# First chunks' state scaling and diagonal sums on ScalarE, and another order of the first steps and loads, in a recurrence plus three-way maximum kernel

## The chip, the cores and the metric

The kernel runs on one core of one Trainium2 chip. The metric is the device time of one execution in microseconds (us), the median of several runs. Five engines run side by side, each through its own list of instructions in order, and wait for one another by semaphores: TensorE (PE, matmuls; PEld is its weight load), VectorE (DVE), ScalarE (ACT), GpSimd (POOL) and SyncE (SP). SyncE and ScalarE also issue the DMA transfers; "SPq" and "ACTq" in a row are such issues or waits in their queues.

## The reference

A gated linear recurrence over 768 time steps for 4 batches and 8 heads of 48 channels, whose output feeds a feed-forward stage:

```python
for t in range(S):
    kt, vt, rt, wt = (k[:, :, t], v[:, :, t], r[:, :, t], w[:, :, t])
    cur = np.einsum('bhd,bhe->bhde', u[None] * kt, vt)
    y[:, :, t] = np.einsum('bhd,bhde->bhe', rt, state + cur)
    state = wt[:, :, :, None] * state + np.einsum('bhd,bhe->bhde', kt, vt)
...
x = attn_out.transpose(0, 2, 1, 3).reshape(B * S, H * D)        # 3072 x 384
h = np.maximum(np.maximum(x @ w1, x @ w2), x @ w3)              # 3072 x 768
return h @ w_out                                                # 3072 x 384
```

## The kernel before

**Tiling.** The 4 x 768 time steps are cut into 24 chunks of 128 steps. Four chunks (512 tokens) make a "half", of which there are six, and the feed-forward stage works on one half at a time. The recurrence inside a chunk is turned into matmuls: a backward and a forward scan of the decays w over the chunk give factors by which k and r are scaled, products of the scaled r and k ("gram") are masked and multiplied with v, and a 48 x 48 state for each head carries over from chunk to chunk.

**Steps of a chunk k**, each one letter: `b` backward scan (and `dec`, a copy of its end values by ScalarE), `s` two small VectorE operations, `f` forward scan, `r` scales r and k, `c` a ScalarE check of the scan's result; `d` products of r and k for the diagonal, `D` their sums by TensorE into a PSUM tile, `e` copies the eight sums out of PSUM (`cs`) and lets GpSimd spread them on the diagonal of the tile `a` (two selections of 64 rows each), and issues the load of the v tile of chunk k+1; `X` the gram matmuls, `M` copies the masked gram into `a` on VectorE, `T` transposes of k and a ScalarE copy of them (`kn`), `R` the state's share of the output y, `U` the new state in PSUM, `S` the state times the next chunk's decays into `sstar`, `V` and `Z` the values in two halves, `E` copies y into the tile x on ScalarE. After chunk 2 `E` also issues six small DMAs that move rows inside x (three on SyncE's queue, three on ScalarE's), and again after chunk 3. `n` loads the 679 KB of a chunk's inputs in two transfers into one of three buffers. The v tiles have three buffers too, so the load for chunk 4 has to wait until TensorE has read the v tile of chunk 1 for the last time, in `Z` of chunk 1.

**Weights.** 24 tiles of 384 KB (64-bit numbers) come in by the step `w`. A tile is turned into 32-bit numbers in two parts: step `i` does the part of ScalarE (line 303), and VectorE follows with lines 312 and 314. `c` without a number and `p` do the same for the next tile in line, and `p` and `m` then run the matmuls of the feed-forward stage; the first two tiles are multiplied with 384 of the 512 tokens in `p` (line 147), and with the last 128 in `m` (line 155). From the third tile on `m` is line 167. The products of line 147 and 155, of `D`, and of line 167 take turns in three PSUM banks ("psm"); the third weight tile takes the bank that the ScalarE copy of line 130 empties.

**Order.** Nothing is reordered by a scheduler: every engine runs its instructions in the order in which the program writes them, and the string `FRONT` writes the first part, chunks 0 to 3 and the start of the feed-forward stage, by hand. `W` with a number is that many dummy matmuls. From chunk 4 on another string sets the order, and a loop lays chunks between the groups of feed-forward matmuls.

Of the kernel before, what the change touches and what calls it, by code (L numbers as in the profile page):

```python
# [34 lines left out]
ALU = mybir.AluOpType  # L35
AF = mybir.ActivationFunctionType
# [4 lines left out]
B, H, S, D = 4, 8, 768, 48  # L41
DM, FF = 384, 768
NP = 4
# [10 lines left out]
CPH = HT // C  # L54
# [12 lines left out]

FRONT = ("b0 s0 f0 d0 W2 D0 W3 r0 X0 T0 W3 c0 e0 b1 s1 d1 D1 U0 f1 W4 R0 e1 M0 V0 Z0 E0 S0 n3 r1 "  # L70
# [3 lines left out]
TURN = "b1 d1 w | f1 w | D1 r1 c1 | e1 M0 w | "  # L74
ORD = "w R0 V0 U0 X1 Z0 E0 b2 d2 | f2 n3 w | D2 S0 r2 c2 | e2 M1 w | T1 w | |"

# [18 lines left out]
def kernel(ctx: ExitStack, tc, tin, nat, u_flat, u_pair, v_t, w_all, out, ytr):  # L95
    nc = tc.nc
# [99 lines left out]
    with ExitStack() as fast:  # L196
# [23 lines left out]
        def load_nat(k):  # L220
            b, c = divmod(k, NCH)
            if k in natt:
                return
            vt = v_p.tile([128, DM], F32, name="v")
            kr = None
            if k >= CS:
                kr = nat_p.tile([128, 2, DM], F32, name="kr")
                nc.sync.dma_start(out=kr[:, :, :], in_=nat[b, c, :, 1:3, :])
            nc.sync.dma_start(out=vt[:, :], in_=nat[b, c, :, 0, :])
            natt[k] = (vt, kr)  # L230
# [39 lines left out]
        sstar = [cst.tile([128, NP, 64], F32, name=f"sstar{i}") for i in range(2)]  # L270
        dec = [cst.tile([128, LINE], F32, name=f"dec{i}")[:, 0:NP] for i in range(2)]
# [83 lines left out]
        prep = {k: {} for k in range(NK)}  # L355
# [59 lines left out]
        def prep_diag2(k):  # L415
            ahead("D", k)
            cs = small.tile([128, LINE], F32, name="cs")[:, 0:H]
            if k < CS:
                nc.vector.tensor_copy(out=cs[:, :], in_=prep[k]["ps"][:, 0:H])
            else:  # L420
                nc.vector.tensor_reduce(out=cs[:, :].rearrange("p (a b) -> p b a", a=2),  # L421
                                        in_=natt[k][1][:, 0, :].rearrange("p (b a d) -> p b a d", a=2, d=D),
                                        axis=AX.X, op=ALU.add)
            a = a_p.tile([128, 4, 3, HC], F32, name="a")
            for lo in (0, HC):
                rows = slice(lo, lo + HC)
                nc.gpsimd.affine_select(out=a[rows, :, 0:2, :], pattern=[[0, 4], [0, 2], [1, HC]],  # L427
                                        in_=cs[rows, :].rearrange("p (a b) -> p a b", b=2).unsqueeze(3).broadcast_to([HC, 4, 2, HC]),
                                        compare_op=ALU.is_equal, fill=0.0, base=0, channel_multiplier=-1)
            prep[k]["a"] = a  # L430
            if k + 1 < NK:
                load_nat(k + 1)
# [28 lines left out]
        def goes_on(k):  # L461
            return k % NCH < NCH - 1
# [36 lines left out]
        def state(k):  # L499

            if goes_on(k):
                new = prep[k]["pu"][0:112, 0:NP * D].rearrange("p (a b) -> p a b", a=NP)
                if k % NCH > 0 and k >= CPH:
                    cur = scur[0:112, :].rearrange("p (a b) -> p a b", a=NP)
                    nc.vector.tensor_tensor(out=cur, in0=new, in1=sstar[k % 2][0:112, :, 0:D], op=ALU.add)
                    new = cur
                nc.vector.tensor_tensor(out=sstar[(k + 1) % 2][0:112, :, 0:D], in0=new,
                                        in1=dec[(k + 1) % 2][0:112, :].unsqueeze(2).broadcast_to([112, NP, D]), op=ALU.mult)

        def after(later, sooner):  # L510

# [27 lines left out]
        def result(k):  # L539
# [11 lines left out]
            for lo in (0, 64) if cols else ():  # L551
                for j in range(KT):
                    eng = nc.scalar if lo and half < PLAIN else nc.sync
                    eng.dma_start(out=x[lo + 48:lo + 64, j, cols], in_=x[lo + 16 * j:lo + 16 * j + 16, KT, cols])  # L554

        steps = dict(X=scores, M=take, T=transposes, R=from_state, U=to_state, S=state, V=values, Z=values2, E=result, n=load,
                     b=prep_scan_b, s=prep_start, f=prep_scan_f, r=prep_rk, c=prep_check, d=prep_diag1,
                     D=prep_diag_sum, e=prep_diag2)
        ready = {("n", k) for k in range(3)}

        def ahead(step, k):

            if k < NK and (step, k) not in ready:
                ready.add((step, k))
                steps[step](k)
# [107 lines left out]
        def take_x(early=False):  # L673
            h = len(xs)
            there = ("E", CPH * (h + 1) - 2) in ready if early else units >= min(UPH * (h + 1) + XD, UPC * NK)
            if h < NH and there and groups >= GPH * h - 2 * CPH:
                xs[h] = x_parts(h)
# [39 lines left out]
        simple = dict(p=part, a=unit, c=weights, i=begin, w=load_w, m=group, f=fix, x=lambda: take_x(True))  # L717
        for step in FRONT.split():
            if step in simple:
# [14 lines left out]
    with tc.If(verdict[0] != 0, label="general"), ExitStack() as slow:  # L734
        pool = lambda name, bufs, **kw: slow.enter_context(tc.tile_pool(name=name, bufs=bufs, **kw))
        c1 = pool("c1", 1)
# [7 lines left out]
        with tc.For_i(0, B) as b:  # L744
            for pr in range(NP):
# [8 lines left out]
                for hh in range(2):  # L754
                    rows = slice(64 * hh, 64 * hh + 48)
                    for t, o in ((wt, pr * WS + 1), (rt, WC + pr * C), (kt, WC + NP * C + pr * C)):
                        for c in range(NCH):
                            for lo in (0, HC):
                                at = o + (HC - lo if t is kt and pr % 2 == 0 else lo)
                                nc.sync.dma_start(out=t[rows, c * C + lo:c * C + lo + HC],  # L760
                                                  in_=tin[ds(b, 1), c, rows, at:at + HC].rearrange("a p n -> (a p) n"))
                    nc.sync.dma_start(out=uc[rows, :], in_=u_pair[pr, hh])
                nc.vector.tensor_scalar(out=uk[0:112, :], in0=kt[0:112, :], scalar1=uc[0:112, :], scalar2=None, op0=ALU.mult)
                for j in range(KT):
                    with tc.For_i(0, 16) as i:
# [5 lines left out]
                        for hh in range(2):  # L771
                            nc.sync.dma_start(
                                out=vb[64 * hh:64 * hh + 48, :],
                                in_=v_t[ds(b, 1), 2 * pr + hh, ds(i + 16 * j, 1), :].rearrange("a e t -> (a e) t").broadcast_to([48, S]))
# [22 lines left out]
        for i in range(NW if w_all.dtype != F32 else 0):  # L797
# [5 lines left out]
            low, scale = raw[:, 0:2 * PC:2], sc[:, :].bitcast(F32)  # L803
# [16 lines left out]
        with tc.For_i(0, NH) as half:  # L820
            x = xs_p.tile([128, KT, HT], F32, name="x")
# [73 lines left out]
```

## Time and profile before

| | |
|---|---|
| time before, median of 3 runs (lowest to highest) | 417.63 us (417.21 to 419.69) |
| the profiled execution's own time | 414.51 us |
| its span in the trace | 412.8 us |
| TensorE busy in the span | 401.7 us (97%) |
| VectorE, ScalarE, GpSimd busy | 277.7, 151.4, 75.0 us |
| DMA bytes moved in the span | 53.30 MB |

The span runs from the first to the last instruction in the trace; 1.7 us of the profiled execution lie outside it. Busy times of engines overlap, so they don't add up; a matmul's end is modelled, so that a TensorE that is shown as busy may still be held up a little. Names such as `w`, `x`, `tin` are the program's tiles, L and a number a line of the kernel before.

### The profile page before, as it was taken

Reading aid. Unit: us, or ns where it says so; the run is one execution under the profiler, and the core shown is the slowest. Engines: PE = TensorE matmul, PEld = TensorE weight load, DVE = VectorE, ACT = ScalarE, POOL = GpSimd, SP = SyncE. Lnnn points to the kernel's source line nnn. Section 1 sums busy time; section 2 is a strip of 40 time slices with the busy share of each in tenths; the row PEclk is TensorE's granted clock in tenths of the full one; section 3 lists DMA queues with packets and bytes.
Section 4 is the critical chain, followed back from the end, with each engine's and each line's share of the span. In section 5 each row is a group of like instructions: output and inputs, shape, how many; then the busy total and the mean of one; then the engine's idle time right before and its main releaser. Section 6 shows DMA issues by size and latency. Waiting matters only on the chain.

```text
span 412.8 us, 9220 instructions
## 1 busy us (share of the span) xinstructions
PE 401.7 (97%) x3761; PEld 316.2 (77%) x3761; DVE 277.7 (67%) x515; ACT 151.4 (37%) x318; POOL 75.0 (18%) x92
## 2 busy tenths in 40 slices
PE   6989999999999999999999999999999999999995
PEld 3666454556688889988889988889988888978894
DVE  6999997878869959748877648777656622233320
ACT  1344333233525543525533635433622321412211
POOL 3311011033231311312221212322122200000000
PEclk9999999999999999999999999999999999999999
DMA  8695973641460321494564595751550000300002
GB/s 208 172 318 170 332 212 129 206 142 40 133 195 4 123 61 67 131 310 123 181 192 123 146 278 178 242 155 62 157 189 2 2 2 0 97 1 2 1 4 76
DMA packets 23838, 53.30 MB, mean 129 GB/s; under 512 B 3280, under 2 KB 9744, under 8 KB 23792
## 3 DMA queue, kind: packets, MB, share of 16 engines
q1 hardware_dynamic: 19872, 42.65, 34.0%
q10 hardware_dynamic: 3920, 10.03, 8.0%
q8 instruction: 30, 0.49, 0.5%
q14 instruction: 16, 0.13, 0.1%
HBM read 46.77 MB, written 4.72 MB: 125 GB/s over the span
## 4 chain that ended last, share of the span: by engine, by line
PE 89%; DVE 4%; DMA 2%; ACT 1%; issue 1%; ACTq 1%; SPq 1%; DVEq 0%; POOLq 0%
PE psm L167 56%; PE psm L187 16%; PE gram L449 4%; PE y L527 4%; PE tu L492 3%; PE y L482 2%; PE tu L469 2%; PE psm L147 1%; DMA out_dram<-m 1%; DVE gf L360 1%; DMA tin<-in_tin_dram 1%; ACTq L554 1%; PE psm L411 1%; DVE kr L399 1%; SPq L554 1%
## 5 line engine op out<-in xcount | busy, mean ns | idle before, releaser
L167 PE MATMUL psm<-x_hi,w 128*128 128x512 f32 x540 | 172.8, 394 | 0.2 <-ACT m L191 0.2
L167 PEld LDWEIGHTS psm<-x_hi,w 128*128 128x128 f32 x540 | 101.3, 188 | 22.3 <-ACT m L191 0.8
L167 PE MATMUL psm<-x_lo,w 128*128 128x512 f32 x270 | 105.3, 390 | 0.0
L133 DVE TENSOR_TENSOR m<-psm,m 128x512 f32<-128x512 f32 x60 | 41.1, 685 | 58.7 <-PE psm L167 42.4
L187 PE MATMUL psm<-w,h_hi 128*128 128x384 f32 x288 | 78.1, 364 | 0.0
L427 POOL TENSOR_SCALAR_AFFINE_SELECT a<-cs 64x512 f32<-64x512 f32 x48 | 36.1, 753 | 157.5 <-DVE cs L421 80.4
L167 PEld LDWEIGHTS psm<-x_lo,w 128*128 128x128 f32 x270 | 50.7, 188 | 9.8
L187 PEld LDWEIGHTS psm<-w,h_hi 128*128 128x128 f32 x288 | 51.7, 188 | 6.5 <-DVE w L314 0.4
L167 PE MATMUL psm<-x,w 128*128 128x512 f32 x96 | 43.1, 599 | 0.0
L545 ACT COPY x<-y 112x512 f32<-112x512 f32 x24 | 14.1, 587 | 76.3 <-PE y L527 75.9
L187 PE MATMUL psm<-w,h_lo 128*128 128x384 f32 x120 | 40.3, 335 | 0.0
L110 ACT CAST h_hi<-m 128x512 fp32r<-128x512 f32 x30 | 18.6, 622 | 54.8 <-DVE m L133 54.4
L391 ACT ACTIVATE gf<-gf 112x1034 f32<-112x1034 f32 x24 | 25.6, 1069 | 34.4 <-DVE tin L386 34.0
L374 DVE TENSOR_TENSOR_SCAN gf<-tin,d_fwd 112x517 f32<-112x517 f32 x24 | 36.5, 1519 | 0.7
L402 POOL TENSOR_TENSOR kr<-kr 128x384 f32<-128x384 f32 x16 | 17.9, 1119 | 92.6 <-PE y L527 76.7
L167 PEld LDWEIGHTS psm<-x,w 128*128 128x128 f32 x96 | 17.6, 190 | 19.5 <-issue 18.9
L360 DVE TENSOR_TENSOR_SCAN gf<-tin,d_bwd 112x517 f32<-112x517 f32 x24 | 29.9, 1246 | 3.7 <-DMA tin<-in_tin_dram 3.7
L111 DVE TENSOR_TENSOR h_lo<-m,h_hi 128x512 fp32r<-128x512 f32 x30 | 20.6, 688 | 17.0 <-ACT h_hi L110 17.0
L527 PE MATMUL y<-a,v 64*48 64x64 f32 (+3 forms) x768 | 25.7, 246 | 0.5
L458 DVE COPY_PREDICATED a<-mask,gram 128x384 f32<-128x384 int32 x48 | 25.3, 582 | 0.5 <-PE gram L449 0.5
L527 PEld LDWEIGHTS y<-a,v 64*64 64x64 f32 (+1 forms) x768 | 21.6, 126 | 4.7 <-issue 2.1
L130 ACT COPY m<-psm 128x512 f32<-128x512 f32 x30 | 17.5, 582 | 15.7 <-PE psm L167 11.0
(72 smaller groups left out, 422.7 us busy)
## 6 DMA issues: line engine op xcount, KB each, us to landing
tin<-in_tin_dram SPq DMA_DIRECT2D x23, 448.0 KB, 5.1
w<-in_w_all_dram SPq DMA_DIRECT2D x24, 384.0 KB, 7.2
cv<-in_w_all_dram ACTq DMA_DIRECT2D x24, 384.0 KB, 3.6
kr<-in_nat_dram SPq DMA_DIRECT2D x16, 384.0 KB, 5.5
tin<-in_tin_dram SPq DMA_DIRECT2D x23, 231.0 KB, 4.1
v<-in_nat_dram SPq DMA_DIRECT2D x24, 192.0 KB, 5.7
out_dram<-m SPq DMA_DIRECT2D x24, 192.0 KB, 2.3
x<-x SPq DMA_DIRECT2D x30, 32.0 KB, 2.0
```

The source lines that it names most:

```text
L110: nc.scalar.copy(out=hi, in_=src)
L111: rest = lambda: nc.vector.tensor_tensor(out=lo, in0=src, in1=hi.bitcast(F32), op=ALU.subtract)
L133: nc.vector.tensor_tensor(out=m[:, :], in0=ps[:, :], in1=m[:, :], op=ALU.max)
L167: nc.tensor.matmul(ps[:, :], lhsT=wt[f * 3 + wi][:, ct * 128:(ct + 1) * 128], rhs=xt[:, ct, :], start=(n == 0), stop=(n == KT * len(terms) ...
L187: nc.tensor.matmul(pss[tt][:, 0:DM], lhsT=ht[f][:, tok], rhs=wt[FT * 3 + f][:, :], start=(f == 0 and i == 0), stop=(f == FT - 1 and i == l ...
L360: nc.vector.tensor_tensor_scan(out=gf[0:112, 0, ::-1], data0=t[0:112, 0:WC][:, ::-1], data1=d_bwd[0:112, ::-1], initial=0.0, op0=ALU.mult, ...
L374: nc.vector.tensor_tensor_scan(out=gf[0:112, 1, :], data0=tbuf[k % NB][0:112, 0:WC], data1=d_fwd[0:112, :], initial=0.0, op0=ALU.mult, op1 ...
L391: nc.scalar.activation(out=flat, in_=flat, func=AF.Square, accum_out=acc[0:112, k:k + 1])
L402: nc.gpsimd.tensor_tensor(out=n[:, 0, :], in0=n[:, 0, :], in1=n[:, 1, :], op=ALU.mult)
L427: nc.gpsimd.affine_select(out=a[rows, :, 0:2, :], pattern=[[0, 4], [0, 2], [1, HC]], in_=cs[rows, :].rearrange("p (a b) -> p a b", b=2).un ...
L458: nc.vector.copy_predicated(out=p["a"][:, 2 * hh:2 * hh + 2, :, :].rearrange("p a b c -> p a (b c)"), mask=mask_b(2), data=p["gs"][hh].rea ...
L527: mm = nc.tensor.matmul(p["y"][64 * half:64 * half + m, hh, j, HC * late:C], lhsT=natt[k][0][lo:lo + HC, h * D:h * D + m], rhs=a[:, j, :] ...
```

## The change

The copy of the eight diagonal sums (`cs`, chunks 0 to 7) goes from VectorE to ScalarE. The scaling of the state for chunks 0 to 3 goes from one VectorE operation to four ScalarE activations of 48 columns, with the decay as scale. `FRONT` is written in another order.

```diff
-FRONT = ("b0 s0 f0 d0 W2 D0 W3 r0 X0 T0 W3 c0 e0 b1 s1 d1 D1 U0 f1 W4 R0 e1 M0 V0 Z0 E0 S0 n3 r1 "
-         "W2 X1 d2 D2 T1 c1 b2 s2 e2 R1 U1 M1 V1 Z1 E1 f2 S1 n4 w w w r2 "
-         "W4 X2 d3 D3 T2 c2 b3 s3 e3 w w R2 U2 n5 i i i M2 V2 Z2 E2 f3 S2 r3 "
-         "W3 X3 d4 T3 R3 M3 x V3 Z3 E3 w w U3 p p w w c n6 w m D4 b4 s4 c c3 S3 m w f4 c e4 m r4 c X4 T4 R4 c4 w w")
+FRONT = ("b0 s0 f0 d0 W2 D0 W3 r0 X0 e0 T0 W3 c0 b1 s1 d1 D1 U0 f1 W4 R0 e1 S0 M0 V0 Z0 E0 n3 r1 "
+         "W2 X1 d2 D2 e2 T1 c1 b2 s2 R1 U1 S1 M1 V1 Z1 E1 f2 r2 "
+         "W4 X2 d3 D3 e3 n4 T2 c2 b3 s3 w w w R2 U2 S2 i i i M2 V2 Z2 E2 w n5 f3 r3 "
+         "W3 X3 d4 T3 R3 M3 x V3 Z3 E3 w w w U3 p p w c n6 w m D4 b4 s4 c c3 S3 m w f4 c e4 m r4 c X4 T4 R4 c4 w w")
...
             if k < CS:
-                nc.vector.tensor_copy(out=cs[:, :], in_=prep[k]["ps"][:, 0:H])
+                nc.scalar.copy(out=cs[:, :], in_=prep[k]["ps"][:, 0:H])
...
-                nc.vector.tensor_tensor(out=sstar[(k + 1) % 2][0:112, :, 0:D], in0=new,
-                                        in1=dec[(k + 1) % 2][0:112, :].unsqueeze(2).broadcast_to([112, NP, D]), op=ALU.mult)
+                for pr in range(NP) if k < CPH else ():
+                    nc.scalar.activation(out=sstar[(k + 1) % 2][0:112, pr, 0:D], in_=new[:, pr, :], func=AF.Identity,
+                                         scale=dec[(k + 1) % 2][0:112, pr:pr + 1])
+                if k >= CPH:
+                    nc.vector.tensor_tensor(out=sstar[(k + 1) % 2][0:112, :, 0:D], in0=new,
+                                            in1=dec[(k + 1) % 2][0:112, :].unsqueeze(2).broadcast_to([112, NP, D]), op=ALU.mult)
```

SyncE's queue after the loads of chunk 3, where `v` is the tile of one chunk, `tin_115` and `tin_116` take the inputs of chunks 4 and 5, `w` is a weight tile, and `x<-x 16x384` and `16x128` are the row moves after chunks 2 and 3 (lines 554 and 558 are the same line before and now):

```order
-L229 DMA v<-in_nat_dram 128x384
+L229 DMA v<-in_nat_dram 128x384 x2
 L241 DMA tin_115<-in_tin_dram 112x528
 L241 DMA tin_115<-in_tin_dram 112x1024
 L287 DMA w<-in_w_all_dram 128x384 x3
-L229 DMA v<-in_nat_dram 128x384
-L287 DMA w<-in_w_all_dram 128x384 x2
+L558 DMA x<-x 16x384 x3
+L287 DMA w<-in_w_all_dram 128x384
 L241 DMA tin_116<-in_tin_dram 112x528
 L241 DMA tin_116<-in_tin_dram 112x1024
-L554 DMA x<-x 16x384 x3
```

The v tile of chunk 4 stood behind chunk 4's inputs and three weight tiles and stands ahead of them now; of the next two weight tiles one stands behind the row moves of chunk 2 now, with the inputs of chunk 5, and the other (not in this piece) behind the row moves of chunk 3.

ScalarE in chunk 2 before, from the decays of chunk 3 (`dec_138`) to the copy of y (L545, which is L549 now); `cv` is ScalarE's part of a weight tile, and DMAHW and a number a counter that a finished transfer raises:

```order
L362 COPY dec_138<-gf 112x4 [waits DVE_49]
L303 ACTIVATE cv<-w,minus_two 128x384 [waits DMAHW0_49]
L303 ACTIVATE cv<-w,minus_two 128x384 [waits DMAHW1_49]
L303 ACTIVATE cv<-w,minus_two 128x384 [waits DMAHW2_49]
L545 COPY x<-y 112x4x128 [waits PE_49]
```

And now:

```order
L362 COPY dec_138<-gf 112x4 [waits DVE_49]
L508 ACTIVATE sstar_136<-tu,dec_138 112x48 [waits PE_49,Activation_49]
L508 ACTIVATE sstar_136<-tu,dec_138 112x48 x3
L303 ACTIVATE cv<-w,minus_two 128x384 [waits DMAHW1_49]
L303 ACTIVATE cv<-w,minus_two 128x384 [waits DMAHW2_49]
L303 ACTIVATE cv<-w,minus_two 128x384 [waits DMAHW3_49]
L549 COPY x<-y 112x4x128 [waits PE_49]
```

The state's four activations moved in ahead of the three weight tiles; the copy of y stands behind the same three as before.

ScalarE after the row moves of chunk 3, now: the fourth and fifth weight tile (`cv`), between them the decays of chunk 4, then the check of chunk 3, its state, and the copy that empties the first psm bank (L130). Before, the state's activations were not in this row, and the rest stood in the same order.

```order
L303 ACTIVATE cv<-w,minus_two 128x384 [waits DMAHW2_49,DVE_49]
L362 COPY dec_137<-gf 112x4 [waits DVE_49]
L303 ACTIVATE cv<-w,minus_two 128x384 [waits DMAHW3_49]
L391 ACTIVATE gf,acc<-gf 112x1034
L508 ACTIVATE sstar_135<-tu,dec_137 112x48 [waits PE_49,Activation_49]
L508 ACTIVATE sstar_135<-tu,dec_137 112x48 x3
L130 COPY h_hi<-psm 128x512 [waits PE_49]
```

The four activations moved in between the check and the copy, and the second `cv` waits for a weight tile whose load moved behind the row moves of chunk 3.

## Rows read from the trace of the kernel before

**Rows 1.** Busy time in stretches: span us, busy (instructions), granted clock, DMA share, GB/s.

```profile
33.70:40.00 6.30, 6.30 (x43) 4.43 (x42) 5.73 (x12) 3.48 (x7) 0.25 (x1) 1.00 0.65 200
...
200.00:300.00 100.00, 100.00 (x962) 87.27 (x961) 71.00 (x131) 46.19 (x106) 23.02 (x26) 1.00 0.56 166
```

**Rows 2.** Chain that ended last, start to 70 us: start, length, what.

```profile
28.40 0.60 ACT x L545
...
30.55 1.35 ACTq L554
...
31.95 0.54 ACT kn L471
...
33.87 3.87 PE psm L147 x12
```

**Rows 3.** SyncE queue, timeline 0 to 48 us: start, length, line, transfer, count.

```profile
18.34 0.78 SPq L241 DMA_DIRECT2D tin<-in_tin_dram  x2
19.18 1.38 SPq L287 DMA_DIRECT2D w<-in_w_all_dram  x3
21.01 0.33 SPq L229 DMA_DIRECT2D v<-in_nat_dram  x1
...
24.68 0.81 SPq L241 DMA_DIRECT2D tin<-in_tin_dram  x2
...
34.91 2.01 SPq L287 DMA_DIRECT2D w<-in_w_all_dram  x4
```

**Rows 4.** VectorE, timeline 0 to 42 us: start, length, line, operation.

```profile
8.89 0.16 DVE L419 COPY cs<-psm 128x8 f32<-128x8 f32 x1
8.97 1.22 DVE L360 TENSOR_TENSOR_SCAN gf<-tin,d_bwd 112x517 f32<-112x517 f32 x1
...
14.06 0.33 DVE L507 TENSOR_TENSOR sstar<-tu,dec 112x192 f32<-112x192 f32 x1
14.31 0.92 DVE L385 TENSOR_TENSOR tin<-tin,gf 112x256 f32<-112x256 f32 x2
...
19.00 1.71 DVE L374 TENSOR_TENSOR_SCAN gf<-tin,d_fwd 112x517 f32<-112x517 f32 x1
```

**Rows 5.** GpSimd, timeline 0 to 42 us.

```profile
9.12 2.26 POOL L427 TENSOR_SCALAR_AFFINE_SELECT a<-cs 64x512 f32<-64x512 f32 x2 [6.01 <-DVE cs L419]
...
18.26 1.37 POOL L427 TENSOR_SCALAR_AFFINE_SELECT a<-cs 64x512 f32<-64x512 f32 x2 [3.63 <-DVE cs L419]
```

**Rows 6.** TensorE, timeline 0 to 48 us.

```profile
19.72 1.23 PE L527 MATMUL y<-a,v 64*64 64x128 f32 x32
...
26.59 0.58 PE L496 MATMUL tu<-sstar,ident 112*112 112x192 f32 x2
...
37.57 0.83 PE L155 MATMUL psm<-x,w 128*128 128x128 f32 x6
...
39.67 2.74 PE L167 MATMUL psm<-x,w 128*128 128x512 f32 x6
```

**Rows 7.** DMA issues beginning at 19.6-20.1, 20.1-20.7, 34.9-35.3, 25.05-25.5: count, size, us to landing.

```profile
w<-in_w_all_dram SPq DMA_DIRECT2D x1, 384.0 KB, 6.3
...
w<-in_w_all_dram SPq DMA_DIRECT2D x1, 384.0 KB, 6.8
...
w<-in_w_all_dram SPq DMA_DIRECT2D x1, 384.0 KB, 3.4
...
tin<-in_tin_dram SPq DMA_DIRECT2D x1, 448.0 KB, 6.9
```

**Rows 8.** ScalarE and its DMA queue, timeline 0 to 42 us.

```profile
25.94 1.72 ACT L303 ACTIVATE cv<-w,minus_two 128x384 f32<-128x384 uint32 x3
...
33.10 2.05 ACTq L554 DMA_DIRECT2D x<-x  x3
...
36.45 1.05 ACT L391 ACTIVATE gf<-gf 112x1034 f32<-112x1034 f32 x1
...
38.44 0.59 ACT L130 COPY h_hi<-psm 128x512 f32<-128x512 f32 x1 [0.85 <-PE psm L155]
```

## The prediction

> **What bounds the kernel now.** I read the busy time by stretch first. From 33.70 us to 395 us TensorE is busy for all but about 0.4 us of 361 us, at the full granted clock [rows 1]. No other engine can shorten that part, and a delay of its start, or a new gap in it, goes to the end in full. So the question is where 33.70 comes from. The chain of waits answers that [rows 2]: the first feed-forward matmul (line 147) follows the new state of chunk 3, which follows the ScalarE copy `kn` at 31.95, and that copy had its input long before: it stood behind the three row moves that ScalarE issues after the copy of y of chunk 2 (28.40). Their last issue took 1.35 us and ended at 31.90. It ends with a transfer: the second half of chunk 5's inputs was issued at about 25.1 and landed 6.9 us later, at 32.0 [rows 3, 7]. So the front of the kernel ends in ScalarE's list, and y of chunk 2 and the transfers in flight matter there. Ahead of it, up to 29 us, VectorE works nearly without a gap.
>
> The third view is SyncE's queue [rows 3]. The inputs of chunk 4 go out at 18.34, three weight tiles at 19.18 to 20.5, the v tile of chunk 4 at 21.01. The last is the moment when `Z` of chunk 1 ends (19.72 + 1.23 = 20.95) [rows 6], on which this transfer waits.
>
> **The change part by part.**
>
> *VectorE's relief.* A copy of sums costs VectorE 0.08 us (8.89 to 8.97), a state 0.25 (14.06 to 14.31) [rows 4]. Three of each before `r` of chunk 3 make 1.0 us, and 0.4 us of that lies ahead of `Z` of chunk 1. Against it stands GpSimd. A selection started at 9.12 under a scan took 2.26 us for the pair, against 1.37 undisturbed [rows 5], and the scan at 19.00, under a selection, took 1.71 instead of 1.22 [rows 4]. The two engines hold each other up by about half a microsecond a chunk. The earlier selections still meet VectorE work, of another kind: chunk 0's now falls under the last product of `r` and the scan. I bound the change in this loss by plus and minus 0.7 us, and take 0.
>
> The Trainium skill ("SBUF — State Buffer", "Who interferes with whom") says that a VectorE instruction with two SBUF inputs and a GpSimd instruction that reads SBUF lock each other out for a whole instruction, while a VectorE instruction with one SBUF input does not. The two scans above agree with it. By it chunk 0's two selections could cost VectorE up to 1.3 us, and those of chunks 2 and 3 less than before, since they would fall more on the masked copies, which read PSUM.
>
> *ScalarE's load.* Four activations a state: no row has one of 48 columns with a scale read from a tile. The nearest rows bound a step by 0.1 us (a four-column copy, 25.86 to the next at 25.94) and 0.54 us (384 columns, three in 1.72 with 0.64 for the last) [rows 8]; near the small end I take 0.22, so 0.9 us a state. The states of chunks 0 and 1 lie in ScalarE's gaps; that of chunk 2 now stands ahead of three weight conversions, that of chunk 3 ahead of the copy that empties the first psm bank.
>
> The Trainium skill ("ScalarE: Activation LUTs", "What ACT_TABLE_LOAD costs" and "Rules for kernel authors") sends plain products to VectorE, and has a step of 0.226 us for such an activation after the overlap; with it a state would be 1.0 us, 0.1 more than my value.
>
> *The loads.* This decides. The v tile of chunk 4 now stands ahead of chunk 4's inputs and the first three weight tiles in SyncE's list, so all of them wait for `Z` of chunk 1. I take that at 0.3 us earlier than before, 20.7 (19.9 if all of VectorE's saving and none of the collisions arrive, 21.3 if the collisions win). Before, from the first issue at 18.34 to the third weight tile's landing passed 20.1 + 6.8 - 18.34 = 8.6 us for 1831 KB [rows 3, 7]. The v tile's 192 KB in front add 0.45 (about half of the 0.95 us between the landings of the second and the third weight tile, 25.95 and 26.9). So the third weight tile lands at 20.7 + 9.05 = 29.75, not 26.9. Before, ScalarE converted the three at 25.94 to 27.66 without a wait [rows 8], and 0.7 us later y of chunk 2 came. Now the third conversion begins at 29.8, and the copy of y, next in the list, at 30.35 instead of 28.40: 1.95 later.
>
> *The row moves and the first matmul.* No load is under way when ScalarE issues the row moves of chunk 2, since the weights have landed, and the inputs of chunk 5 are put behind the moves. The same three issues took 2.05 us after chunk 3 with quiet DMA engines [rows 8] and 2.9 here (28.99 to 31.90); I take 2.05. So `kn` begins at 30.35 + 0.6 + 2.05 + 0.1 = 33.1, 1.15 later, and the first matmul at 34.85.
>
> *The third weight tile's matmuls.* SyncE's list now has, behind the row moves of chunk 2, the fourth weight tile (at 32.8) and chunk 5's inputs, then the row moves of chunk 3 (which wait for ScalarE's copy, done at 33.1 + 0.53 + 0.6 = 34.2, and take to 36.0), then the fifth weight tile at 36.05; before, the fifth had been issued by 22.3. Ahead of its landing 1447 KB have to come: before, this amount took 7.6 us from idle (18.34 to 19.65 + 6.3 = 25.95), so 40.4. The floor is 36.05 + 3.4, a weight tile's time from idle at 34.91 [rows 7], so 39.45. I take the middle, 39.9. ScalarE's list then has the conversion (0.54), the check of chunk 3 (1.0 to 1.05), the state (0.9) and the copy of line 130 (0.59) [rows 8]: done at 42.95. The matmuls of the third weight tile need the bank that this copy empties, so they begin at 43.05 instead of 39.67 [rows 6]: 3.4 later. TensorE has done everything ahead of them by then: the matmuls of line 155 began at 37.57 and would at 38.7, 2.1 ahead of line 167. The 1.15 us is in the 3.4. Afterwards the weight tiles come faster than TensorE uses them (2.74 us each [rows 6]; the third landed 0.95 us after the second), so I add nothing.
>
> Sum: 414.51 + 3.4 = 417.9 for a profiled execution. The median of the runs before stands 3.12 us above the profiled execution; I carry that over: 417.63 + 3.4 = 421.0, 0.8% more. About 1% is what a measurement of this kernel can tell from no change.
>
> **The rivals.**
>
> *The loads land in time.* If the DMA engines, idle at 20.7, deliver the 2023 KB some 2 us faster, the gap closes and the change does what the relief promises. `I`, the last matmul of chunk 2's state, ended at 27.17 [rows 6]; with 0.7 us of VectorE's saving 26.5, the state on ScalarE to 27.35, three conversions to 29.0, y of chunk 2 then 0.6 later than before, the row moves 0.85 shorter: the first matmul 0.25 earlier, and up to 1.0 earlier if TensorE's own gap ahead of `I` closes. About 417.0. For it speaks that the queue is empty then; against it that 8.6 us were measured from an empty queue as well.
>
> *The row moves of chunk 3 stall.* Before, the third row move of chunk 2 ended as chunk 5's inputs landed. Now chunk 5's inputs stand ahead of the moves of chunk 3. If the issue waits for them again, until 32.8 + 5.6 = 38.4 (1063 KB at the pace of 1447 KB in 7.6 us), the fifth weight tile goes out at 38.45, lands 3.4 later at 41.85, and line 167 comes 1.95 us later than above: 5.35 later, 423.0, slower by 1.3%. The point from which it decides: an issue of the moves of chunk 3 on SyncE over 1 us. Against it: each move of chunk 3 is 8 KB instead of 24.
>
> *The change doesn't do what it says.* VectorE's saved time could be all idle time, since TensorE's list of chunk 1 runs on its own from `Z` of chunk 0 with dummy matmuls in it. Then the 0.3 us at `Z` of chunk 1 is lost: 421.3, inside the forecast.
>
> **How the numbers follow.** Forecast (late loads, with the last rival) 0.57, loads in time 0.23, stall 0.20. The forecast's own range is 419.0 to 422.8, from 39.45 less 0.8 us for an early `Z` to 40.4 plus 0.6 for a late one, with some room for the conversions. The whole range reaches from 416.7 (loads in time, the gap closed in part) to 423.2 (the stall). Slower by over 1%, above 421.8: the stall and a quarter of the forecast, 0.33. Faster by over 1% needs 4 us, more than all of VectorE's saving: 0.02. Within 1%: 0.65.
>
> **What would show it.** In the profile of the changed kernel: the v tile of chunk 4 issued near 20.7 and the weight tiles behind it; ScalarE idle ahead of the third conversion with a weight transfer as the releaser; the copy of y of chunk 2 at about 30.4; the row moves after it in about 2 us; `kn` near 33.1; a wait of TensorE ahead of line 167 on the copy of line 130, which follows a wait for the fifth weight tile. Wrong would be: conversions without a wait, a first matmul ahead of 33.7, or gaps in TensorE's work after 45 us, which would mean that later weight tiles or the inputs of chunk 6 come too late; I have put nothing on that.

## The result, and the profile after

The changed kernel takes 421.50 us in the median of 5 runs (420.38 to 422.17); the kernel before, with two more runs, 417.21 (414.37 to 419.69). The ratio is 1.0116, interval 1.0084 to 1.0148: slower by 1.2% (the two medians alone give 1.0103). The profiled execution of after took 422.14 us, its span is 420.4 us. The two profiled executions differ by 7.6 us and the medians by 4.3, because the one of before lies at the low end of its runs and the one of after near the top of its own. One of the runs below, of the kernel before with after's loads, took 2251.05 us, is counted as slow and stands in no number of this text.

SyncE's queue of after, timeline: start, length, line, transfer, count.

```profile
15.48 5.77 SPq L229 DMA_DIRECT2D v<-in_nat_dram  x2
21.34 1.70 SPq L241 DMA_DIRECT2D tin<-in_tin_dram  x2
23.08 1.38 SPq L287 DMA_DIRECT2D w<-in_w_all_dram  x3
...
33.42 2.12 SPq L241 DMA_DIRECT2D tin<-in_tin_dram  x2
36.35 1.78 SPq L558 DMA_DIRECT2D x<-x  x3
38.19 2.22 SPq L287 DMA_DIRECT2D w<-in_w_all_dram  x4
```

The two v tiles are one row now: the second, chunk 4's, waits for `Z` of chunk 1 and goes out at about 20.9. Chunk 4's inputs follow 3.0 us, the first weight tile 3.9 us later than in [rows 3]. The fifth weight tile is the first of the last row, at 38.19.

The chain that ended last, cut: start, length, what.

```profile
24.03 5.64 DMA w<-in_w_all_dram
...
30.24 0.57 ACT x L549
...
33.42 4.74 DMA tin<-in_tin_dram
...
38.19 4.09 DMA w<-in_w_all_dram
...
44.75 0.48 ACT h_hi L130
...
45.28 4.40 PE psm L167 x6
```

Against [rows 2], where ScalarE's list carried the front, it is now transfers: the third weight tile until 29.67, then the first part of chunk 5's inputs until 38.17, and right behind its landing the fifth weight tile, until 42.28. ScalarE and its DMA queue, timeline (in brackets: idle time ahead, and what ended it):

```profile
25.62 0.88 ACT L508 ACTIVATE sstar<-tu,dec 112x48 f32<-112x48 f32 x4 [0.18 <-PE tu L496]
27.63 0.66 ACT L303 ACTIVATE cv<-w,minus_two 128x384 f32<-128x384 uint32 x1 [1.14 <-DMA w<-in_w_all_dram]
28.78 0.64 ACT L303 ACTIVATE cv<-w,minus_two 128x384 f32<-128x384 uint32 x1 [0.48 <-DMA w<-in_w_all_dram]
29.69 0.64 ACT L303 ACTIVATE cv<-w,minus_two 128x384 f32<-128x384 uint32 x1 [0.27 <-DMA w<-in_w_all_dram]
...
30.83 2.17 ACTq L558 DMA_DIRECT2D x<-x  x3
33.04 0.53 ACT L471 COPY kn<-tu 128x448 f32<-128x448 f32 x1 [2.24 <-issue]
...
34.09 2.10 ACTq L558 DMA_DIRECT2D x<-x  x3
...
42.30 0.64 ACT L303 ACTIVATE cv<-w,minus_two 128x384 f32<-128x384 uint32 x1 [4.00 <-DMA w<-in_w_all_dram]
...
43.89 0.86 ACT L508 ACTIVATE sstar<-tu,dec 112x48 f32<-112x48 f32 x4
```

The three conversions, one group without a wait in [rows 8], wait three times for weights, and the next after chunk 3 waits 4.00 us. TensorE, timeline, and stretches of the span (span us, busy and count of PE, PEld, DVE, ACT, POOL, granted clock, DMA share, GB/s):

```profile
24.35 0.67 PE L492 MATMUL tu<-v,kn 128*64 128x48 f32 x16
...
30.85 0.66 PE L482 MATMUL y<-tin,sstar 48*64 48x128 f32 x16 [2.05 <-ACT x L549]
...
35.42 5.42 PE L147 MATMUL psm<-x,w 128*128 128x384 f32 x12
...
45.28 4.40 PE L167 MATMUL psm<-x,w 128*128 128x512 f32 x6 [2.34 <-ACT h_hi L130]
```

```profile
31.00:32.00 1.00, 1.00 (x32) 0.96 (x28) 1.00 (x2) 0.00 (x0) 0.00 (x0) 0.70 0.00 0
33.70:36.00 2.30, 2.30 (x19) 1.96 (x20) 0.44 (x3) 0.36 (x1) 0.00 (x0) 0.50 0.81 255
...
44.00:46.00 2.00, 0.72 (x1) 0.50 (x2) 0.86 (x3) 2.00 (x8) 0.11 (x1) 0.76 1.03 320
46.00:48.00 2.00, 2.00 (x3) 0.67 (x2) 2.00 (x3) 0.45 (x1) 1.56 (x2) 0.50 1.07 217
```

The gap of 2.05 us is that behind the late copy of y; before line 167 stands a second one of 2.34. After both, the granted clock is 0.50, the 1.2 GHz level, where [rows 1] has 1.00: twelve matmuls of line 147 take 5.42 us (4.04 at the full clock, in a run below), six of line 167 take 4.40 (2.74 in [rows 6]). Line 167 begins 5.6 us and ends 7.3 us later than before, and this stays to the end (7.6).

VectorE was relieved, but where nothing came of it. `Z` of chunk 1 ended at 20.83, 0.1 us earlier than in [rows 6]; the scan at 18.62 takes 1.51 us (1.71 in [rows 4]), and chunk 1's backward scan pays for chunk 0's selections, which start ahead of it now (at 8.90):

```profile
8.97 1.68 DVE L360 TENSOR_TENSOR_SCAN gf<-tin,d_bwd 112x517 f32<-112x517 f32 x1
...
18.62 1.51 DVE L374 TENSOR_TENSOR_SCAN gf<-tin,d_fwd 112x517 f32<-112x517 f32 x1
```

The same scan took 1.22 in [rows 4]. That agrees with the rule of the Trainium skill ("SBUF — State Buffer", "Who interferes with whom") which the prediction weighed.

### The profile page after: what moved, and what is told of

Its sections match the earlier page's. It is cut to its first block, busy times and chain, and to the rows that moved or that the text cites. A ratio compares the mean times of both kernels' runs of the same rounds, so it can differ in the third digit from the quotient of the medians.

```text
span 420.4 us, 9240 instructions
## 1 busy us (share of the span) xinstructions
PE 405.7 (96%) x3761; PEld 318.5 (76%) x3761; DVE 275.3 (65%) x503; ACT 155.7 (37%) x342; POOL 76.5 (18%) x92
## 4 chain that ended last, share of the span: by engine, by line
PE 84%; DMA 6%; DVE 4%; ACT 2%; SPq 2%; issue 1%; ACTq 0%; DVEq 0%; POOLq 0%
PE psm L167 55%; PE psm L187 16%; PE gram L449 4%; PE y L531 3%; PE y L482 2%; DMA w<-in_w_all_dram 2%; PE tu L492 2%; DMA tin<-in_tin_dram 2%; PE tu L469 1%; SPq L558 1%; DMA out_dram<-m 1%; DVE gf L360 1%; DVE gf L374 1%; DVE tin L385 1%; DVE tin L386 1%
## 5 line engine op out<-in xcount | busy, mean ns | idle before, releaser
L167 PEld LDWEIGHTS psm<-x_hi,w 128*128 128x128 f32 x540 | 101.4, 188 | 22.5 <-ACT m L191 0.8
L427 POOL TENSOR_SCALAR_AFFINE_SELECT a<-cs 64x512 f32<-64x512 f32 x48 | 37.9, 789 | 164.1 <-DVE cs L421 72.9
L167 PE MATMUL psm<-x,w 128*128 128x512 f32 x96 | 44.8, 618 | 2.3 <-ACT h_hi L130 2.3
L549 ACT COPY x<-y 112x512 f32<-112x512 f32 x24 | 14.1, 586 | 71.7 <-PE y L531 71.3
L374 DVE TENSOR_TENSOR_SCAN gf<-tin,d_fwd 112x517 f32<-112x517 f32 x24 | 35.4, 1473 | 0.7
L130 ACT COPY m<-psm 128x512 f32<-128x512 f32 x30 | 17.5, 582 | 15.1 <-PE psm L167 11.0
```

What stands on the lines that cost most here:

```text
L167: nc.tensor.matmul(ps[:, :], lhsT=wt[f * 3 + wi][:, ct * 128:(ct + 1) * 128], rhs=xt[:, ct, :], start=(n == 0), stop=(n == KT * len(terms) ...
L374: nc.vector.tensor_tensor_scan(out=gf[0:112, 1, :], data0=tbuf[k % NB][0:112, 0:WC], data1=d_fwd[0:112, :], initial=0.0, op0=ALU.mult, op1 ...
```

## The experiments

The theory on record is that the loads make the loss, in two places: the first three weight tiles, and the fifth. Its rival is ScalarE's added work. All ratios are to the kernel before, run beside them on the same chip (medians 416.31, 416.28 and 416.68 us in the three groups). A difference in us between two changed kernels is one of medians; where the two are of different groups, the ratios make it up to 0.5 us smaller.

**Loads as before, all else as after.**

```diff
-f2 r2 ... e3 n4 T2 c2 b3 s3 w w w R2 U2 S2 ... E2 w n5 f3 ... E3 w w w U3 p p w c n6
+f2 n4 w w w r2 ... e3 w w T2 c2 b3 s3 R2 U2 n5 S2 ... E2 f3 ... E3 w w U3 p p w w c n6
```

> The changed kernel with only its loads in the order of before (chunk 4's inputs and three weight tiles ahead of the v tile of chunk 4, two more weight tiles and chunk 5's inputs ahead of the row moves of chunk 2); the copies and states stay on ScalarE and the selections early. Late loads (my theory): the three conversions follow the state of chunk 2 (ends at 26.5 us in the changed kernel) without a wait for a transfer, y of chunk 2 is copied near 28.2, the first feed-forward matmul (line 147) starts at 33.7 within 0.4, line 167 at 39.7 within 0.5, the granted clock stays at 1.00 there; time within 1 us of before, 3.5 to 5 us less than the changed kernel. Rival, ScalarE's added work (a state of 0.88 us ahead of the conversions, another ahead of the copy of line 130): the time stays above 420, since none of that is undone.

415.87 us (413.97 to 418.19), ratio 0.9984 (0.9954 to 1.0014). The loss is gone with the loads, so ScalarE's part doesn't make it. The times foretold inside the front missed: the profiled execution is the longest of the twelve (418.19 us). The conversions wait for no transfer in it, but TensorE has a gap that no wait explains, the granted clock is 0.50 behind it, y of chunk 2 is copied at 30.41 and line 147 begins 2.4 us later than in before (the stretch behind the rows has its columns in the order given above):

```profile
26.66 0.40 PE L492 MATMUL tu<-v,kn 128*64 128x48 f32 x3 [1.69 <-issue]
...
36.14 4.04 PE L147 MATMUL psm<-x,w 128*128 128x384 f32 x12
```

```profile
25.70:32.50 6.80, 5.72 (x72) 3.76 (x72) 2.22 (x6) 2.93 (x8) 0.00 (x0) 0.50 0.69 217
```

**Before, with after's loads alone.**

```diff
-E1 f2 S1 n4 w w w r2 ... s3 e3 w w R2 U2 n5 i i i ... E2 f3 S2 ... E3 w w U3 p p w w c n6
+E1 f2 S1 r2 ... s3 e3 n4 w w w R2 U2 i i i ... E2 w n5 f3 S2 ... E3 w w w U3 p p w c n6
```

> The kernel before with only the loads in the changed order; copies and states on VectorE as before. Late loads: y of chunk 2 at 30 us or later after waits of ScalarE for weight transfers, line 167 at 45 or later after a wait on the copy of line 130, the granted clock at half in places between 30 and 50 us; time 420.5 to 422.5, as the changed kernel or a little above, since VectorE's relief is missing. Rival, ScalarE's added work: as before, 417 within 1 us.

420.51 us (median of seven runs), ratio 1.0099 (1.0065 to 1.0134): the loads alone make a loss that can't be told from after's. ScalarE waits for the third weight tile and the fifth:

```profile
31.97 0.64 ACT L303 ACTIVATE cv<-w,minus_two 128x384 f32<-128x384 uint32 x1 [1.25 <-DMA w<-in_w_all_dram]
...
44.04 0.65 ACT L303 ACTIVATE cv<-w,minus_two 128x384 f32<-128x384 uint32 x1 [3.06 <-DMA w<-in_w_all_dram]
```

**After, with the v tile of chunk 4 alone put behind the three weight tiles.**

```diff
-e3 n4 T2 c2 b3 s3 w w w R2          (e3 loads the v tile of chunk 4)
+e3 n4 T2 c2 b3 s3 w w w v4 R2       (step v4 loads it)
```

> The changed kernel with one transfer moved: the v tile of chunk 4 behind the first three weight tiles. Late loads in two parts: chunk 4's inputs go out near 18.3, the three conversions wait for nothing, y of chunk 2 near 28.2, its row moves take about 2.1 us as no load is under way, first matmul at 32.5 to 33.2, earlier than before; but the fifth weight tile still stands behind the row moves of chunk 3, goes out near 36, and line 167 starts near 42.5 after a wait on the copy of line 130, 2.5 to 3.5 later than before: time 419 to 420.5. Rival, the first three weight tiles are all of it: line 167 near 39, time 416 to 417.

419.20 us, ratio 1.0062 (1.0034 to 1.0090). The conversions run without a wait, and the copy of y of chunk 2 comes at 29.12 instead of 30.24 (28.2 was foretold; line 492 has a gap of 1.14 us here, too). The fifth weight tile is still awaited for 3.12 us, and TensorE waits for 2.35 ahead of line 167, here with no fall of its clock:

```profile
43.58 2.84 PE L167 MATMUL psm<-x,w 128*128 128x512 f32 x6 [2.35 <-ACT h_hi L130]
```

So the v tile is one part of the loss, not all.

**After, with the fourth and fifth weight tile right behind the first three.**

```diff
-s3 w w w R2 U2 S2 ... E2 w n5 ... 
+s3 w w w w w R2 U2 S2 ... E2 n5 ...
```

> The changed kernel with the fourth and fifth weight tile loaded right behind the first three, ahead of the row moves of chunk 2, and nothing else moved. Late loads in two parts: the first matmul stays near 35.4 or comes up to 0.5 later (two tiles under way during the row moves), the copy of line 130 waits for no weight tile, line 167 starts within 1 us of the end of line 155's matmuls, near 43, and runs at the full clock: 2.3 us of waiting and 1.6 us of half clock gone, time 417 to 418.5. Rival, the row moves of chunk 3 behind chunk 5's inputs cause the second wait: line 167 still at 44 or later, time above 420.

418.58 us, ratio 1.0049 (1.0024 to 1.0075). The wait for the fifth tile is gone and line 167 begins at 43.47 without a wait; what is left is the first part, the third conversion at 30.22, a gap of 2.67 us and the lower clock behind it:

```profile
35.95 5.58 PE L147 MATMUL psm<-x,w 128*128 128x384 f32 x12
```

**After, with the three weight tiles ahead of the v tile of chunk 4, and the next two behind chunk 4's inputs.** In after almost nothing is transferred from 17 to 21 us (a share of 0.07); the weight tiles have buffers of their own and need not wait for `Z`.

```diff
-c1 b2 s2 R1 ... n4 T2 c2 b3 s3 w w w R2 U2 S2 i i i M2 V2 Z2 E2 w n5 ... E3 w w w U3 p p w c n6
+c1 b2 s2 w w w R1 ... n4 T2 c2 b3 s3 w w R2 U2 S2 i i i M2 V2 Z2 E2 n5 ... E3 w w U3 p p w w c n6
```

> After, with the first three weight tiles issued ahead of the v tile of chunk 4, right behind the v tile of chunk 3 (about 16 us, when the transfers of the trace of after are idle from 17 to 21 us), the fourth and fifth behind chunk 4's inputs, and chunk 5's inputs alone behind the row moves. Late loads: the three weight tiles land by about 21, ScalarE converts them without a wait right after the state of chunk 2 (about 26.4 to 28.1), the copy of y of chunk 2 is at about 28.1 against 30.24, the first feed-forward matmul at about 32.8 against 35.42, line 167 without a wait of TensorE near 39, about 0.5 us below the kernel before in the median, 0.5 to 2 below. Rival, ScalarE's added work is the cost: the states and sums stay where they are, so 419 or more. If the instruction transfer of TensorE falls behind the weight data again, a gap of 0.7 to 1.7 us in the state matmuls (line 492) of chunk 2 shows it, and 0.5 to 1.5 us are lost of that.

413.67 us (413.40 to 414.05), ratio 0.9936 (0.9909 to 0.9962): 7.8 us under after, with the same instructions in the same order on every engine but SyncE. The times foretold for ScalarE and TensorE are within 0.2 us of the trace; the third weight tile landed at 22.34, not at about 21, still 4 us ahead of its conversion, and the median is 2.6 us below before's, more than the 0.5 to 2 foretold. No fall of the clock and no unexplained gap:

```profile
32.65 4.04 PE L147 MATMUL psm<-x,w 128*128 128x384 f32 x12
...
39.15 2.74 PE L167 MATMUL psm<-x,w 128*128 128x512 f32 x6
```

**The same, with the conversions ahead of the copy of the transposed k of chunk 2.**

```diff
-e3 n4 T2 c2 b3 s3 w w R2 U2 S2 i i i M2
+e3 n4 i i i T2 c2 b3 s3 w w R2 U2 S2 M2
```

> As the run before, with the three conversions on ScalarE also ahead of the copy of the transposed k of chunk 2, so that the copy of y of chunk 2 follows the state at once. Late loads: y at about 27, the first matmul at about 31.5, 1.3 us less than the run before and 2 to 3 us less than the kernel before. Rival, chunk 3's scaling of r and k on VectorE (ended at 27.24 in after) or TensorE's transposes of chunk 3 become the bound: the first matmul not before 32, gain at most 0.7 over the run before. Rival, ScalarE's conversions there hold up the copy of the transposed k of chunk 2 and with it the state: gain none.

415.80 us, ratio 0.9982 (0.9952 to 1.0012). The third possibility happened: TensorE waits 1.23 us for that copy, and the copy of y comes at 28.07, no earlier than without the edit. The 2.1 us by which the median is above the run before are more than its profiled execution shows (414.49). Its two runs above 418 us have a mean granted clock of 0.986, the five below 415 us 0.997 or 0.998, so the long ones ran in part at the lower clock; at which place, no trace shows.

**After, with eight dummy matmuls in the gap ahead of `R` of chunk 3.**

```diff
-X3 d4 T3 R3
+X3 d4 T3 W8 R3
```

> After with eight dummy matmuls on TensorE in its 2.05 us gap ahead of R of chunk 3. If the cost of the lower TensorE clock from 31 to 38 us is hidden behind the wait for the fifth weight tile: the first feed-forward matmuls (line 147) take about 4.0 instead of 5.4 us, the wait ahead of line 167 grows by as much, and the time is that of after within 0.5 us. If the lower clock there is what costs: 1.5 to 2 us less than after, about 419.7.

420.65 us, ratio 1.0096 (1.0060 to 1.0132). It didn't do what it was for: the third weight tile came later in this execution (its conversion at 31.31), 1.88 us of the gap stayed, and the clock fell to 0.50 all the same. But it tests the point from the other side. Line 147 began 1.6 us later than in after and took 0.6 longer; the wait ahead of line 167 shrank by 1.3, and its start moved by 1.0, as the conversion of the fifth weight tile did (43.26, in after 42.30):

```profile
37.06 6.01 PE L147 MATMUL psm<-x,w 128*128 128x384 f32 x12
...
46.24 2.84 PE L167 MATMUL psm<-x,w 128*128 128x512 f32 x6 [1.07 <-ACT h_hi L130]
```

Line 167 follows the fifth weight tile, and a slow line 147 is hidden behind it. With a wait of 1.07 us ahead of it, line 167 runs at the full clock here (2.84 us) with no dummies of its own.

**After, with dummy matmuls in both gaps.**

```diff
-X3 d4 T3 R3 ... f4 c e4 m r4
+X3 d4 T3 W8 R3 ... f4 c e4 G10 m r4     (G10: ten dummy matmuls into a gram bank)
```

> After with dummy matmuls in both gaps of TensorE, eight ahead of R of chunk 3 and ten ahead of line 167. Hidden clock in the first part: line 167 still begins at about 45.3 after the copy of line 130, but its six matmuls take 2.74 instead of 4.40 us: 1.6 us less than after, about 419.9, still 3 us over the kernel before. If all of the lower clock counts: 3.6 less, about 418. If the clock costs nothing in the end: 421.5.

420.32 us, ratio 1.0094 (1.0057 to 1.0132). The six matmuls of line 167 take 2.82 us instead of 4.40 and start at 45.64. In the trace the tile ends 1.2 us earlier than in after; the medians differ by 1.2 as well, but the two intervals overlap, and this kernel's can't be told from the one before it, whose line 167 ran at the full clock without them. So the second fall of the clock costs 1.6 us at line 167 in the trace of after, 1.2 in the end by the medians, which don't settle it; and without it most of the loss is still there. The fifth weight tile is issued at 39.51, after SyncE had waited for 0.9 us (SyncE's waits from 38.6 to 39.6 us: line, what it waited for, us in total, times, longest):

```profile
SPq L287 <- DMA tin<-in_tin_dram: 0.9, 1, 0.9
```

**Before, with the loads of the 413.67 us run.**

```diff
-e2 R1 ... f2 S1 n4 w w w r2 ... e3 w w R2 U2 n5 i i i ... E2 f3 S2
+e2 w w w R1 ... f2 S1 r2 ... e3 n4 w w R2 U2 i i i ... E2 n5 f3 S2
```

> The kernel before (states and diagonal sums on VectorE, its order of the steps) with the loads in the order of the run with the weights ahead of the v tile of chunk 4 (413.67 us). Late loads are all: ScalarE's part of the change is worth little either way, so 413.2 to 414.7, and TensorE has no gap in the state matmuls (line 492) of chunk 2, since no data is in flight when its instructions come (before: a gap of 0.75 us, and an instruction transfer between 23 and 24 us; here it should lie between 19 and 22). Rival, VectorE's relief is what the earlier loads let through: without it 1 us or more above 413.67, so 414.7 or more. If the gap in line 492 stays with the instruction transfer early, the gap isn't the instruction transfer's.

414.28 us, ratio 0.9941 (0.9922 to 0.9959). With the same loads, states and sums on VectorE cost 0.6 us more than on ScalarE (0.2 by the ratios), inside the intervals: that part of the change can't be told from nothing. The gap inside line 492, 0.75 us before, is gone (before first, then this kernel):

```profile
26.37 0.29 PE L492 MATMUL tu<-v,kn 128*48 128x48 f32 x2 [0.75 <-issue]
```

```profile
24.73 0.82 PE L492 MATMUL tu<-v,kn 128*64 128x48 f32 x16
```

**The 413.67 us run, with the fifth weight tile alone as far back in the queue as in after.**

```diff
-s3 w w R2 U2 S2 ... E3 w w U3 p p w w c n6
+s3 w R2 U2 S2 ... E3 w w w U3 p p w c n6
```

> The run with the weights ahead of the v tile of chunk 4 (413.67 us), with the fifth weight tile alone put back to where after has it, behind the row moves of chunk 3. Late fifth tile as a cost of its own: it is issued at about 34.8, lands at 38.3 to 39.5, so the conversion, check, state and the copy of line 130 end near 42.3 and line 167 begins near 42.4 instead of 39.15: 3.2 us more without a fall of TensorE's clock, 4.8 with one, 417 to 418.5. Rival, the later part has slack that takes it up: 414.

417.90 us, ratio 1.0024 (0.9998 to 1.0050), 4.2 above that run. Landing and conversion came as expected, line 167 at 41.27, 1.1 earlier than expected, but at the lower clock. The chain shows what the tile's issue waited for:

```profile
30.73 4.13 DMA tin<-in_tin_dram
...
34.88 3.39 DMA w<-in_w_all_dram
```

```profile
38.29 0.64 ACT L303 ACTIVATE cv<-w,minus_two 128x384 f32<-128x384 uint32 x1 [2.79 <-DMA w<-in_w_all_dram]
```

```profile
41.27 4.41 PE L167 MATMUL psm<-x,w 128*128 128x512 f32 x6 [2.16 <-ACT h_hi L130]
```

**The 413.67 us run, with the conversions behind the copy of y of chunk 1.**

```diff
-Z1 E1 f2 r2 ... U2 S2 i i i M2
+Z1 E1 i i i f2 r2 ... U2 S2 M2
```

> The run with the weights ahead of the v tile of chunk 4 (413.67 us), with the three conversions on ScalarE right behind the copy of y of chunk 1 (21.0 to 21.6), in ScalarE's idle 1.8 us there. If ScalarE's list still bounds the front: the copy of y of chunk 2 at 26.8 instead of 28.1, the copy kn of chunk 3 at 29.7 instead of 31.05, the first feed-forward matmul at 31.8 instead of 32.65, 0.8 less, 412.9. Rival, the third weight tile lands later than 22 us, and the sum of chunk 3 and the copy of the transposed k of chunk 2 wait behind its conversion, as in the run with the conversions ahead of that copy: 414 to 416.

413.49 us (412.81 to 414.74), ratio 0.9924 (0.9895 to 0.9953), the fastest median of all, 0.2 us below the run it starts from, which the intervals don't separate. The copy of y of chunk 2 came 1.3 earlier, at 26.82, but 0.9 of this went to the row moves behind it, which took 3.13 us instead of 2.26, and line 147 began only 0.4 earlier, at 32.21 (31.8 foretold):

```profile
27.44 3.13 ACTq L558 DMA_DIRECT2D x<-x  x3
30.62 0.53 ACT L471 COPY kn<-tu 128x448 f32<-128x448 f32 x1 [3.21 <-issue]
```

## Why the prediction was right, and where it was not

**Right: the first half.** The loads behind the v tile decide, as foretold. The third weight tile landed at 29.67 (29.75 foretold), y of chunk 2 was copied at 30.24 (30.35), the row moves took 2.17 (2.05), `kn` began at 33.04 (33.1). Each new state cost ScalarE 0.86 to 0.88 us (0.9). Of VectorE's relief 0.1 us arrived at `Z` of chunk 1 (0.3 taken) and none at the end; putting v alone back took 2.3 us off, and putting the loads back took the loss away.

**Mis-sized: the fifth weight tile.** Foretold was its issue at 36.05, landing at 39.9, line 167 at 43.05. It was issued at 38.19, landed at 42.28, and line 167 began at 45.28. The step that failed is the issue, which the sum puts at the end of the row moves of chunk 3 and gives no wait. The issues ahead of it took longer: chunk 5's inputs went out in 2.12 us, not in the 0.81 of [rows 3], and then SyncE waited for 0.7 us until a row move had landed, so the row moves of chunk 3 began at 36.35, not 34.25 (SyncE's waits from 35 to 37 us, and its waits for TensorE left out):

```profile
SPq L558 <- DMA x<-x: 0.7, 1, 0.7
```

But shorter issues would have changed little. The last row move's issue ended at 38.13, and the fifth weight tile waits for a counter that the first part of chunk 5's inputs raises when it lands, which was at 38.17. In all six traces with the fifth tile behind the row moves of chunk 3 its issue begins 0.01 to 0.02 us after that landing: in after, with after's loads alone, with the v tile behind, with the fifth tile alone late, and in the two with dummies, where SyncE had stood idle for 0.6 and 0.9 us. With after's loads alone the issues of chunk 5's inputs took 0.83 us, and the tile waited all the same. So this is the rival of the stalled row moves in mechanism as in its times (issue 38.45, landing 41.85, line 167 5.35 us later, against 38.19, 42.28 and 5.6), one place further back: its point of decision, a row move's issue of over 1 us, wasn't met, for each took under 0.6 us, and the wait for chunk 5's inputs stood at the weight tile itself. With the three first tiles early and only the fifth late, 4.2 us came back (3.7 by the ratios), so this is a cost of its own; the first three alone (the run with the fourth and fifth early) cost 4.9 (4.7) against the same kernel. Together they are 9.1 where after shows 7.8 (8.4 and 7.5): the later start of line 147 is in part hidden behind the wait for the fifth tile.

**Missed: the clock.** All durations were taken at the full clock of [rows 1], with no reason given for it behind a gap. Line 147 began at 35.42 (34.85 foretold), since the state's matmuls ahead of it took 2.1 us instead of 1.4; it was 1.4 us longer and line 167 1.7 us longer than in before, at 0.50. The first is hidden in the wait for the fifth tile; the second is not.

**Missed: what the medians of before hold.** I carried over 3.12 us from before's profiled execution to its median. After had nothing of the kind (its median is 0.64 below its profiled time). So the median came out at 421.5, near 421.0, by two errors of opposite sign, which is luck: 7.6 us instead of 3.4 in the traces, and 3.1 + 0.6 less on the way from trace to median. What before loses in its longer runs isn't in its trace, but their clocks say where to look. Of its 23 runs in the last group the four below 415.5 us have a mean granted clock of 0.995 to 1.000, the three above 418 us 0.990 or 0.991; the profiled execution has 1.000. So the longer runs went in part at the lower clock. The kernel with before's loads shows one such execution in its trace (418.19 us, 0.990): the unexplained gap of 1.69 us in line 492 and 0.50 behind it. The kernel of before with early weights, where loads alone are changed, has 0.996 to 1.000 in all its twelve runs, and they range over 2.4 us (413.19 to 415.58) where before's range over 4.4 (414.57 to 419.00). That before's longer runs have this same gap, which is 0.75 us in its one trace, is argued and not shown.

**One reading of before that isn't shown.** The last row-move issue on ScalarE is said to end with the landing of chunk 5's inputs. It ended at 31.90, as SyncE's did, and the inputs landed at 31.99, so the landing didn't end it; what did is open.

**The rivals.** That the loads land in time fell: ScalarE waited for all three. ScalarE's added work as the cause fell in two runs (loads back, and loads alone). The stall came, at another issue than the one named. That VectorE's saved time is idle time nearly held: 0.1 us of it reached `Z` of chunk 1.

## What to carry to other kernels

Where a load has to wait for a buffer, look at what stands behind it in its queue: here a v tile of 192 KB held up three weight tiles that had buffers of their own, and putting these ahead of it, into a stretch where the transfers were idle, and the next two right behind chunk 4's inputs, made 7.8 us with no other engine's list changed. Ask of each issue, too, which earlier transfer has to land first: the fifth weight tile stood behind the landing of inputs that it had nothing to do with. Moving work from a busy engine to an idle one was worth at most 0.6 us beside that. Give an issue a range from several rows, not one time, and compare a profiled execution with the spread of its runs and their clocks before a difference to the median is carried over.

## What the runs showed of the hardware that was not expected

**The clock falls after gaps of TensorE, not after each of them.** It went to 0.50 after gaps of 2.05 and 2.34 us (after), 1.88 and 1.67 (what the dummies left of the first gap; a second one of 1.1 stands behind each), 2.16 (late fifth tile), 1.69 (loads as before), 2.67 (fourth and fifth tile early) and 3.02 (after's loads alone). It stayed at 1.00 after 0.75 (before), 0.76 (weights ahead), 1.07 (dummies in the first gap), 1.23 (conversions ahead of the copy of k) and, in the kernel with the v tile behind, after 1.14 and 2.35. So a gap's length alone doesn't decide. With dummies in the second gap it stayed at 1.00; that they kept it there isn't shown, since it also did after the 2.35.

**A gap of TensorE comes with a late instruction transfer.** Each of the 13 traces has one instruction transfer on the queue q8 between 19 and 25 us. In the three kernels that issue chunk 4's inputs and weight tiles from about 18 us on (before, loads as before, v tile behind) it begins between 23.25 and 24.25, and the gap inside line 492 ends 2.4 to 2.7 us behind that in all three (at 26.37, 26.66 and 25.86). In nine of the other ten it begins between 19.75 and 21.75, and in the kernel of before with early weights at 22.5, and there is no such gap. Of before at 23.75 to 24.00, and of that kernel at 22.50 to 22.75 (queue: packets, MB, share):

```profile
q8 instruction: 1, 0.02, 26.7%
```

```profile
q8 instruction: 1, 0.02, 31.9%
```

That the gap is TensorE waiting for these instructions is inferred. Beside the times one thing speaks for it: counted over all records of TensorE in the trace, the first matmul behind the gap is the 707th in all three, though this block of line 492 begins two records earlier in before. That the gap goes when the loads are moved is shown.

**An issue has no fixed length.** The two issues of chunk 5's inputs took 0.83 us (after's loads alone), 1.00 (weights ahead), 2.12 (after) and 2.54 (v tile behind). Three row moves took 2.17 us on ScalarE with the weights landed and 3.13 with loads under way, but also 2.10 with loads under way (after, at 34.09; the transfers' share is 0.81 there). Of after's long issues one fell beside ScalarE's row moves; the other, of chunk 4's inputs, did not, for ScalarE issued nothing then:

```profile
33.91 1.63 SPq L241 DMA_DIRECT2D tin<-in_tin_dram  x1
```

```profile
21.77 1.26 SPq L241 DMA_DIRECT2D tin<-in_tin_dram  x1
```

So neither the other queue nor the transfers under way are shown to be the cause; it is open.
